# Moving ScalarE's preparation of heads and chunks to other places of an attention iteration

## The chip, the cores and the metric

The kernel runs on one core of one Trainium2 chip. A core has a matrix engine (TensorE, PE in the profile, with its weight loads as PEld), a vector engine (VectorE, DVE), an activation engine (ScalarE, ACT), a general engine (GpSimd, POOL), and a sync engine (SyncE, SP) that issues nearly all DMA transfers here. Each engine takes its own instructions strictly in the order of the program; they wait for one another through semaphores. The metric is the device time of one execution in microseconds. The median of several runs is compared.

## The reference

Three stages follow one another. The first is attention in which each query keeps only its 32 largest scores:

```python
scores = scale * np.matmul(q, k.transpose(0, 1, 3, 2))          # B, H, S, D = 4, 8, 576, 64
kth = np.partition(scores, -32, axis=-1)[..., -32:-31]
attn = softmax(np.where(scores >= kth, scores, -1e9))
x = np.matmul(attn, v)                                          # to (2304, 512)
h = x @ w_in                                                    # d_ff = 2048
x = (np.maximum(h, 0) + alpha * np.minimum(h, 0)) @ w_out
logits = x @ w_gate + modality_bias[modality_id]                # 8 experts, one for each token
out[mask] = gate_w * (np.maximum(x[mask] @ w1[e], 0) @ w2[e])   # F = 1024
```

## The kernel before, in words

Matrix products need more precision than one f16 holds, so an operand is scaled by a power of two and split into a high f16 part (ScalarE copies) and a low f16 part (GpSimd subtracts). Three products of parts then make one product.

**The iterations.** Attention is worked off in 72 iterations `s_` of two tiles of 128 queries each; an iteration is a pass of the loop in `phase1`. Tile `t` goes through it as a pipeline: its scores and its 32 largest values are found in iteration s (`topk`, VectorE, some 7 us), its mask in s+1 (`mask`: ScalarE writes `u`, line 526, from the thresholds `bc` that GpSimd has made, line 506; GpSimd subtracts, line 527), its exponentials in s+1 too (`expo`, line 530), its high part in s+1 (`high`, line 534), its low part in s+2 (`low`, lines 538 and 539, then a DMA transpose), and its product with V in s+3 (`av`).

**The order written out by hand.** The schedule is manual: the program order is the order on each engine. Within an iteration it is: hooks "early", `bc`, `low` of the tiles of s-2, `mask` of the tiles of s-1, squares and high parts of the FFN's weights (`wgroup.between`, in the first dozen iterations), hooks "next", the first five steps of `topk`, hooks "first", second products of the FFN (`mm2`), `pair` (ScalarE's high part of `g`, line 672, and GpSimd's low part, line 673), the scores of the next tiles, `mm1`, hooks "gap", the rest of `topk`, then on ScalarE `expo` of the first tile, `keep_scores` of the next tiles (line 457, which `topk` of the next iteration waits for), `expo` of the second tile, a copy of FFN values (line 651), `high`, then hooks "mid", `av`, hooks "late", and last the reading of weights (`wgroup`, VectorE, lines 259 to 261, and the weights' low parts, line 280 on GpSimd and 282 on VectorE).

**Preparation of heads.** A pair of heads (b, pr) is prepared once, by the list `c.steps` of `prep`: `load_qk` and `load_v` (SP), `norms_qk` and `norm_v` (ScalarE, line 392), `scales` (a small product on PE, then VectorE and GpSimd), `high_qk` (ScalarE, two instructions for q and two for k, lines 414 and 415), `low_qk` (GpSimd, line 419, two instructions), `high_v` (ScalarE, lines 431 and 432), `turn` (a DMA transpose from SP, line 423), `swap` (two DMAs from SP, line 427), `low_v`, `keep_`. The list `steps0` puts each step in a hook, so many iterations ahead of the pair's first tile: `("late", 4)` is the hook "late" four iterations ahead. Twelve pairs are prepared up to iteration 22, four more for iterations 54 to 63; all other pairs are loaded ready from memory. Before the main loop a short loop runs the hooks of iterations -6 to -2 alone.

**Preparation of chunks.** The output of attention is collected in chunks of 256 tokens for the FFN. A chunk's list `c.pre` puts `norm` (ScalarE, line 609), `scale` (VectorE, line 212, and GpSimd), `high` (ScalarE, lines 617 and 618, four instructions), `low` (GpSimd, line 622) and `turn` (DMA transpose) into hooks of the iterations after the chunk is complete. There are ten chunks; the first has a list of its own, `c.pre0`.

Of the kernel before, what the change touches and what calls it, by code (L numbers as in the profile page):

```python
# [10 lines left out]
F16 = mybir.dt.float16  # L11
# [3 lines left out]
AF = mybir.ActivationFunctionType  # L15
# [45 lines left out]
def tile_kernel(ctx, tc, q, k, v, w_in, w_out, alpha, mod_id, w_gate, mod_bias, w1, w2, out, dbg=None, force=False):  # L61
    nc = tc.nc
    V, A, G, T, SY = nc.vector, nc.scalar, nc.gpsimd, nc.tensor, nc.sync
# [95 lines left out]
    def run(exact):  # L159
        with ExitStack() as rs:  # L160
            rc = rs.enter_context(tc.tile_pool(name="rc", bufs=1))
            flags = None if exact else rc.tile([128, 2 * 144 + NFB], BF16, name="flags")
            ohs = rc.tile([128, E], F16, name="ohs")
            G.memset(ohs, 0.0)
            mp = Rec()
            with tc.manual_schedule():
                with ExitStack() as ph:
                    blk, over = phase1(exact, ph, rc, rs, flags, ohs, mp)
                mp.B = rs.enter_context(tc.tile_pool(name="moeB", bufs=1))
                if exact:  # L170
                    moe_phase(MAXBLK, blk, mp)
                else:
                    units_phase(blk, mp, lambda: doubts(rc, flags, blk, over))
            if not exact:
                return nc.values_load(blk[0:1, 32:33], min_val=0, max_val=(2 * 144 + NFB) * 128 + MAXBLK)


    def phase1(exact, ph, rc, rs, flags, ohs, mp):
        wts = ph.enter_context(tc.tile_pool(name="wts", bufs=1))
        atts = ExitStack()  # L180
        att = atts.enter_context(tc.tile_pool(name="att", bufs=2, side="right"))
# [15 lines left out]
        def hooked(slot, s_):  # L197
            while hooks[slot].get(s_):
                hooks[slot][s_].pop(0)()
# [25 lines left out]
        def flush():  # L225
            while fill:
                fill.pop(0)()
# [113 lines left out]
        def prep(m, b, pr, keep):  # L341

            c = Rec()
# [20 lines left out]
            raws = []  # L364
# [43 lines left out]
                fill.append(lambda: G.tensor_copy(c.sv[:, 0:1], c.s[:, 2:3]))  # L408
                fill.append(lambda: G.tensor_scalar(c.sv[:, 1:2], c.s[:, 2:3], 1e-9, None, op0=ALU.mult))

            def high_qk():
                c.qk = att.tile([128, 2, 9, 128], F16, name="qk", bufs=1)
                for i in range(2):
                    A.activation(raws[i], raws[i], AF.Copy, scale=c.s[:, i:i + 1])
                    A.activation(c.qk[:, i, :, 0:64], raws[i], AF.Copy)

            def low_qk():
                for i in range(2):
# [18 lines left out]
            def keep_():  # L437
                if keep:
                    SY.dma_start(qkD[b * 4 + pr].rearrange("p (s c) -> p s c", c=128), c.QK)
                    SY.dma_start(vvD[b * 4 + pr], c.VV.rearrange("p s c -> p (s c)"))  # L440

            c.steps = [load_qk, load_v, norms_qk, norm_v, scales, high_qk, low_qk, high_v, turn, swap, low_v, keep_]
            return c


# [150 lines left out]
        def chunk(ci, xn, rs):  # L596
            ffn = state.ffn
            c = Rec()
# [12 lines left out]
            def scale():  # L611
                c.s, c.iv = pow2(c.sq[:, :R], R, small, "xs", 5)
# [172 lines left out]
                        b0 = (2 * rs[0] + j) * S + 512  # L785
                        SY.dma_start(x2D[b0:b0 + 64, :], c.x2[64 * j:64 * j + 64, 0, :])

            c.pre = [("late", 0, norm), ("gap", 1, scale), ("late", 1, high), ("mid", 2, low), ("late", 2, turn)]
            c.pre0 = [("late", 0, norm), ("early", 1, lambda: (scale(), flush())), ("next", 1, high), ("gap", 1, low), ("mid", 1, turn)]
            c.mm1, c.relus, c.slope, c.pair, c.mm2 = mm1, relus, slope, pair, mm2  # L790
            c.fin, c.gate1, c.gate2, c.gate3, c.keep, c.place, c.logits, c.weight = fin, gate1, gate2, gate3, keep, place, logits, weight
# [68 lines left out]
        for n_, ts in enumerate(iters):  # L860
            for t in ts:
                first.setdefault(t.m, n_)
        pc = {}
        steps0 = [("next", 6), ("mid", 6), ("late", 6), ("next", 5), ("next", 4), ("late", 4), ("next", 3), ("late", 3),
                  ("late", 3), ("next", 2), ("mid", 2), ("late", 1)]
        seen = set()
        for m, (b, pr) in enumerate(seq):
            places = [("early", 3), ("late", 1)] if (b, pr) in seen else steps0
            seen.add((b, pr))
            for x, (slot, ahead) in enumerate(places):  # L870
                def step(m=m, x=x):
                    if m not in pc:
                        b_, pr_ = seq[m]
                        more = (b_, pr_) in seq[m + 1:]
                        pc[m] = prep(m, b_, pr_, more)
                    pc[m].steps[x]()
                at(slot, first[m] - ahead, step)
# [14 lines left out]
        def wstep(n):  # L892
            if state.out is not None or not n:
                return
            wgroup(n)
            if state.ffn is None and wgroup.cn["square"] == 32 and s_ > LCON[-1][1]:
                state.words.close()
                state.ffn = ph.enter_context(tc.tile_pool(name="ffn", bufs=2))
            if wgroup.cn["low"] == 32:
                state.stage.close()  # L900
                state.out = ph.enter_context(tc.tile_pool(name="ffnout", bufs=2))
# [14 lines left out]
        def start_chunk(ci, rs, s_):  # L916
            if state.ffn is None:
                return at("late", s_ + 1, lambda: start_chunk(ci, rs, s_ + 1))
            xn = xh.rearrange("p r h d -> p r (h d)") if ci == 8 else xns[ci // 2, ci % 2]
            if dbg is not None and exact == force:  # L920
                if ci < 8:
                    SY.dma_start(dbg[0][ci].rearrange("(p r) c -> p r c", r=2), xn)
                else:
                    SY.dma_start(dbg[0][ci].rearrange("(r p) c -> p r c", r=2)[:, rs[0]], xn[:, rs[0]])
            c = chunk(ci, xn, rs)
            c.k = state.started
            state.started += 1
            state.chunk = c
            for slot, x, f in (c.pre if c.k else c.pre0):
                at(slot, s_ + x, f)  # L930
            for fp in range(c.n):
                fpq.append((s_ + XLAT[c.k > 0], c, fp))
# [116 lines left out]
        for s_ in range(min(min(h_) for h_ in hooks.values() if h_), -LOOK):  # L1049
            hooked("early", s_)  # L1050
            wgroup.between(WSTEP)
            hooked("next", s_)
            hooked("mid", s_)
            flush()
            hooked("late", s_)
            wstep(WEARLY.get(s_, 0))
        s_ = -LOOK
        while True:
# [69 lines left out]
            while fpq and credit >= 1 and n_ < 2 and fpq[0][0] <= s_ and weights_for(fpq[0][2]):  # L1128
                credit -= 1
                _, c, fp = fpq.pop(0)  # L1130
# [446 lines left out]
```

## Time and profile before

| what | us |
|---|---|
| median of 3 runs (lowest, highest) | 1145.56 (1140.29, 1146.42) |
| the profiled execution: its time, and its span | 1142.26, 1140.5 |
| busy in the span: PE / DVE / ACT / POOL | 844.8 / 806.0 / 755.4 / 706.2 |
| first score tile on VectorE (iteration 0) | 39.74 |
| iterations 5 to 14 begin (first score instruction on VectorE) | 123.21, ..., 244.38 |
| iterations 23, 49 and 62 begin | 334.17, 553.83, 691.83 |
| last iteration (71) begins | 768.26 |

The span is from the first to the last instruction; the profiled execution's own time is 1.76 us longer. Busy time is an average over stages: after 768 us attention is nearly over and the FFN's end and the expert stage follow. A row of a timeline says when an instruction started, how long it ran, and in brackets how long its engine had stood idle before it and what released it.

### The profile page before, as it was taken

To read this page: it belongs to the slowest core of one execution; us is meant where nothing else is said; L and a number is where in the kernel's file an instruction comes from. 1 tells how busy PE (TensorE), PEld (TensorE's weight loads), DVE (VectorE), ACT (ScalarE), POOL (GpSimd) and SP (SyncE) were. 2 spreads that over 40 slices of the span, in tenths; PEclk is the share of its full clock that TensorE was granted. 3 is DMA by queue.
4 is the path that set the end of the run, shared out by engine and by line. 5 is a ranking of instruction groups with operands and counts; after the bars stand their busy time and mean duration, and the time that the engine had idled before them with its cause. 6 is when DMAs were issued, how large, how long until landed. Compare 5 with 4: busy or idle time off the path is not lost.

```text
span 1140.5 us, 21484 instructions
## 1 busy us (share of the span) xinstructions
PE 844.8 (74%) x7100; PEld 602.5 (53%) x7100; DVE 806.0 (71%) x2813; ACT 755.4 (66%) x1276; POOL 706.2 (62%) x1106
## 2 busy tenths in 40 slices
PE   0202133257779889778887878989999899999995
PEld 0001122135446566555555546657666778888884
DVE  5778778688799999999888879994225333443331
ACT  5466698998987887878888978895325233342441
POOL 3165397899988988988788999897333220230210
PEclk9999565678889999999899989999999999999998
DMA  8979967677795685686798678765104272543420
GB/s 248 257 181 230 269 141 157 160 164 165 169 214 126 133 180 108 132 175 122 138 161 167 154 155 178 161 130 74 19 20 167 93 258 84 176 147 112 130 93 21
DMA packets 297110, 170.21 MB, mean 149 GB/s; under 512 B 245458, under 2 KB 270034, under 8 KB 296988
## 3 DMA queue, kind: packets, MB, share of 16 engines
q1 hardware_dynamic: 293212, 158.24, 59.2%
q0 software_dynamic: 3776, 10.51, 2.5%
q8 instruction: 57, 0.93, 0.4%
q14 instruction: 65, 0.53, 0.2%
HBM read 81.42 MB, written 25.94 MB: 94 GB/s over the span
## 4 chain that ended last, share of the span: by engine, by line
PE 33%; POOL 17%; DVE 17%; ACT 16%; DMA 7%; issue 7%; SPq 2%; POOLq 0%; ACTq 0%
PE psS L1383 9%; PE psX L1366 8%; PE psX L686 6%; POOL HL L538 4%; POOL S L527 4%; PE psS L637 4%; DVE m L477 3%; DVE X L501 3%; ACT S L530 3%; DMA PT<-HL 3%; ACT HL L534 2%; ACT S L457 2%; DVE F L477 2%; DMA rawk<-in_k_dram 2%; ACT u L526 2%
## 5 line engine op out<-in xcount | busy, mean ns | idle before, releaser
L686 PE MATMUL psX<-Wo,g 128*128 128x512 f16 x864 | 218.2, 402 | 50.5 <-POOL g L673 36.0
L527 POOL TENSOR_TENSOR S<-u,S 128x576 f32<-128x576 bf16 x144 | 182.3, 1287 | 49.4 <-ACT u L526 49.2
L637 PEld LDWEIGHTS <-Wi 128*128 128x128 f16 x1920 | 170.9, 99 | 46.0 <-DVE gr L665 14.2
L538 POOL TENSOR_TENSOR HL<-S,HL 128x512 f16<-128x512 f32 x144 | 166.8, 1158 | 25.4 <-ACT HL L534 16.0
L637 PE MATMUL psH<-xT,Wi 128*128 128x256 f16 (+1 forms) x1488 | 158.4, 265 | 12.4 <-DVE gr L665 8.2
L453 PE MATMUL psS<-QK 128*128 128x512 f16 (+1 forms) x160 | 64.2, 439 | 137.4 <-DVE B L471 95.8
L686 PEld LDWEIGHTS <-g 128*128 128x128 f16 x864 | 82.4, 102 | 152.8 <-POOL g L673 46.1
L530 ACT ACTIVATE S<-S,bc,nb 128x576 f32<-128x576 f32 x144 | 124.1, 862 | 41.0 <-POOL S L527 41.0
L453 PEld LDWEIGHTS <-QK 128*128 128x128 f16 (+1 forms) x320 | 32.3, 110 | 196.5 <-issue 60.6
L1392 POOL DMA_INDIRECT out_dram<-o,ids x18 | 21.0, 1165 | 165.7 <-ACT o L1390 162.9
L673 POOL TENSOR_TENSOR g<-gr,g 128x512 f16<-128x512 f32 x72 | 84.0, 1167 | 53.4 <-ACT g L672 47.8
L477 DVE MAX8 m<-X 128x8 f32<-128x160 f32 x432 | 117.0, 312 | 0.0
L526 ACT ACTIVATE u<-S,bc 128x576 bf16<-128x576 f32 x144 | 103.1, 765 | 13.1 <-POOL bc L506 13.0
L1373 DVE SCALAR_TENSOR_TENSOR gl<-psX,gh 128x512 fp32r<-128x512 f32 (+1 forms) x40 | 25.4, 636 | 115.5 <-ACT gh L1372 115.5
L534 ACT ACTIVATE HL<-S 128x576 f16<-128x576 f32 x144 | 91.4, 681 | 15.6 <-DMA PT<-HL 15.6
L1372 ACT ACTIVATE gh<-psX 128x512 fp32r<-128x512 f32 (+1 forms) x40 | 22.3, 557 | 109.6 <-PE psX L1366 109.6
L457 ACT ACTIVATE S<-psS 128x576 f32<-128x576 f32 x144 | 84.2, 634 | 8.0 <-PE psS L454 8.0
L501 DVE MATCH_REPLACE8 X<-m,X 128x160 f32<-128x160 f32 x288 | 86.6, 307 | 0.0
L558 PE MATMUL bankO<-VV,PT 128*128 128x66 f16 (+1 forms) x2240 | 85.4, 199 | 0.0
L558 PEld LDWEIGHTS <-PT 128*128 128x128 f16 (+1 forms) x2240 | 81.8, 105 | 4.8 <-issue 3.5
L474 DVE SCALAR_TENSOR_TENSOR X<-psS,S 128x288 f32<-128x288 f32 (+1 forms) x144 | 80.7, 602 | 2.5
L672 ACT ACTIVATE g<-gr 128x512 f16<-128x512 f32 x72 | 44.9, 624 | 39.8 <-DVE gr L665 23.4
(286 smaller groups left out, 2069.6 us busy)
## 6 DMA issues: line engine op xcount, KB each, us to landing
raw<-in_moe_w_dram SPq DMA_DIRECT2D x40, 512.0 KB
qkD<-QK SPq DMA_DIRECT2D x16, 576.0 KB
QK<-qkD SPq DMA_DIRECT2D x16, 576.0 KB
wraw<-in_moe_w_in_dram SPq DMA_DIRECT2D x16, 512.0 KB
wraw<-in_moe_w_out_dram SPq DMA_DIRECT2D x16, 512.0 KB
vvD<-VV SPq DMA_DIRECT2D x16, 325.0 KB
VV<-vvD SPq DMA_DIRECT2D x16, 325.0 KB
K<-QK SPq DMA_DIRECT2D x32, 144.0 KB
```

What stands on the lines that cost most here:

```text
L457: A.activation(t.S, SC[:, t.z, :S], AF.Copy, scale=LOWER)
L477: ops.append(lambda: V.max(o, a_))
L501: ops.append(lambda i_=i_, r=r: V.match_replace(out=dst(i_), in_to_replace=m[:, i_, 8 * r:8 * r + 8], in_values=src(i_) if r == 0 else dst ...
L526: A.activation(u, t.S, AF.Relu, scale=-BIG, bias=t.cut)
L527: G.tensor_tensor(t.S, u, t.S, op=ALU.subtract)
L530: A.activation(t.S, t.S, AF.Exp, scale=t.c.negc, bias=t.b)
L534: A.activation(t.HL.rearrange("p a b -> p (a b)")[:, 0:S], t.S, AF.Copy)
L538: G.tensor_tensor(f[:, 640:1152], t.S[:, 0:512], f[:, 0:512], op=ALU.subtract)
L558: T.matmul(oo, l, r, start=(n_ == 0), stop=(n_ == len(ops) - 1), skip_group_check=True)
L637: T.matmul(h[:, fb, :], Wi[:, 4 * cc + f0 // 512, wh, f0 % 512:f0 % 512 + 128], c.xT[:, :R, xh_, cc, :], start=(n == 0), stop=(n == 11))
L686: T.matmul(c.X2[r], g[:, gh, fb, r * 128:r * 128 + 128], Wo[:, FB * fp + fb, wh, :], start=(fp == 0 and fb == 0 and n == 0), stop=(fp == c ...
L1383: T.matmul(self.Y[r], g_[:, r * 128:r * 128 + 128], w_[:, j % 2, :], start=(j == 0 and n == 0), stop=(j == 7 and n == 2))
```

## The change

It changes in which hook the steps of preparation stand, and cuts `high_qk` in two (`high_q`, `high_k`, the same four instructions). For a pair of heads the norms of q and k move from the end of iteration -6 to behind the masks of iteration -5, the norm of v from there to "mid" of -5, the high part of q from "late" to "mid" of -4, the high part of k from "late" of -4 to behind the masks of -3, the low parts on GpSimd from "next" to "mid" of -3, the high part of v from "late" of -3 to behind the masks of -2. For a chunk, `norm` and `high` move from "late" to "next" of the following iteration. The loop ahead of the main loop gets one more `flush()`. No instruction is added or removed.

```diff
-            def high_qk():
-                c.qk = att.tile([128, 2, 9, 128], F16, name="qk", bufs=1)
-                for i in range(2):
-                    A.activation(raws[i], raws[i], AF.Copy, scale=c.s[:, i:i + 1])
-                    A.activation(c.qk[:, i, :, 0:64], raws[i], AF.Copy)
+            def high_(i):
+                if i == 0:
+                    c.qk = att.tile([128, 2, 9, 128], F16, name="qk", bufs=1)
+                A.activation(raws[i], raws[i], AF.Copy, scale=c.s[:, i:i + 1])
+                A.activation(c.qk[:, i, :, 0:64], raws[i], AF.Copy)
...
-            c.steps = [load_qk, load_v, norms_qk, norm_v, scales, high_qk, low_qk, high_v, turn, swap, low_v, keep_]
+            c.steps = [load_qk, load_v, norms_qk, norm_v, scales, high_q, high_k, low_qk, turn, high_v, swap, low_v, keep_]
...
-            c.pre = [("late", 0, norm), ("gap", 1, scale), ("late", 1, high), ("mid", 2, low), ("late", 2, turn)]
+            c.pre = [("next", 1, norm), ("gap", 1, scale), ("next", 2, high), ("mid", 2, low), ("late", 2, turn)]
...
-        steps0 = [("next", 6), ("mid", 6), ("late", 6), ("next", 5), ("next", 4), ("late", 4), ("next", 3), ("late", 3),
-                  ("late", 3), ("next", 2), ("mid", 2), ("late", 1)]
+        steps0 = [("next", 6), ("mid", 6), ("next", 5), ("mid", 5), ("next", 4), ("mid", 4), ("next", 3), ("mid", 3),
+                  ("late", 3), ("next", 2), ("next", 2), ("mid", 2), ("late", 1)]
...
             hooked("next", s_)
+            flush()
             hooked("mid", s_)
```

## Rows read from the trace of the kernel before

**Rows 1.** Busy time by stretch: bounds, length, busy (instructions) by engine, PEclk, DMA, GB/s.
```profile
39.74:123.21 83.47, 15.20 (x102) 8.26 (x102) 69.06 (x202) 48.85 (x92) 39.15 (x75) 0.94 0.88 224
123.21:244.38 121.17, 38.29 (x360) 25.96 (x360) 94.47 (x315) 109.50 (x196) 97.73 (x141) 0.59 0.70 170
244.38:334.17 89.79, 66.93 (x600) 41.57 (x600) 75.30 (x298) 80.14 (x135) 82.36 (x121) 0.89 0.77 175
334.17:553.83 219.66, 190.54 (x2013) 128.79 (x2014) 216.57 (x888) 177.68 (x293) 190.91 (x293) 0.98 0.69 143
553.83:691.83 138.00, 111.95 (x1189) 73.82 (x1187) 113.61 (x467) 114.77 (x197) 120.89 (x196) 0.91 0.79 161
```

**Rows 2.** Waits over the span: total us, times, longest.
```profile
POOL S L527 <- ACT u L526: 49.2, 14, 10.7
...
ACT u L526 <- POOL bc L506: 13.0, 9, 2.9
```

**Rows 3.** Timeline of ScalarE from 78 to 95 us.
```profile
78.18 0.76 ACT L414 ACTIVATE rawq<-rawq,scs 128x576 f32<-128x576 f32 x1
...
79.56 0.76 ACT L414 ACTIVATE rawk<-rawk,scs 128x576 f32<-128x576 f32 x1
...
87.40 0.68 ACT L392 ACTIVATE junk<-rawq 128x576 f16<-128x576 f32 x1 [6.37 <-DMA rawq<-in_q_dram]
...
88.99 0.68 ACT L392 ACTIVATE junk<-rawk 128x576 f16<-128x576 f32 x1 [0.81 <-DMA rawk<-in_k_dram]
...
89.67 1.43 ACT L526 ACTIVATE u<-S,bc 128x576 bf16<-128x576 f32 x2
...
94.74 0.85 ACT L530 ACTIVATE S<-S,bc,nb 128x576 f32<-128x576 f32 x1
```

**Rows 4.** Timeline of GpSimd at three of its masks.
```profile
90.51 2.53 POOL L527 TENSOR_TENSOR S<-u,S 128x576 f32<-128x576 bf16 x2 [10.74 <-ACT u L526]
...
563.32 2.53 POOL L527 TENSOR_TENSOR S<-u,S 128x576 f32<-128x576 bf16 x2 [5.29 <-ACT u L526]
...
586.25 2.54 POOL L527 TENSOR_TENSOR S<-u,S 128x576 f32<-128x576 bf16 x2 [2.74 <-ACT u L526]
```

**Rows 5.** Timeline of ScalarE from 557 to 566 us.
```profile
557.15 0.68 ACT L392 ACTIVATE junk<-rawq 128x576 f16<-128x576 f32 x1 [1.02 <-DMA rawq<-in_q_dram]
...
559.93 0.71 ACT L617 ACTIVATE xn<-xn,xss 128x512 f32<-128x512 f32 x1
...
562.48 1.42 ACT L526 ACTIVATE u<-S,bc 128x576 bf16<-128x576 f32 x2
...
565.05 0.85 ACT L530 ACTIVATE S<-S,bc,nb 128x576 f32<-128x576 f32 x1
```

**Rows 6.** Timeline of SP's queue, ScalarE and VectorE in the start.
```profile
20.89 4.44 SPq L423 DMA_TRANSPOSE QK<-qk  x1
...
21.77 0.63 ACT L266 ACTIVATE junk<-Wi 128x512 f16<-128x512 f32 x1
...
39.74 0.47 DVE L474 SCALAR_TENSOR_TENSOR psS<-psS,S 128x288 f32<-128x288 f32 x1 [5.52 <-ACT S L457]
```

**Rows 7.** Timeline of ScalarE, GpSimd and VectorE from 652 to 657 us.
```profile
652.59 0.77 ACT L414 ACTIVATE rawq<-rawq,scs 128x576 f32<-128x576 f32 x1
...
654.97 0.20 POOL L506 TENSOR_TENSOR bc<-m,nb 128x4 f32<-128x4 f32 x1
...
655.37 0.61 ACT L609 ACTIVATE xjunk<-xn 128x512 f16<-128x512 f32 x1
...
656.11 0.15 DVE L212 TENSOR_SCALAR xsk<-xsq 128x1 int32<-128x1 int32 x1 [1.10 <-ACT xjunk L609]
...
656.74 1.43 ACT L526 ACTIVATE u<-S,bc 128x576 bf16<-128x576 f32 x2
```

**Rows 8.** Two lines' instructions: duration ns least/median/most, first and last start.
```profile
L419 POOL TENSOR_TENSOR qk<-rawq,qk x16: 1272/1280/1767, 18.2 to 660.5; 128x576 f16<-128x576 f32 x16
...
L282 DVE SCALAR_TENSOR_TENSOR Wi<-Wi,wp0s x6: 750/751/1778, 134.2 to 163.7; 128x512 f16<-128x512 f32 x6
```

More of the change, by code (lines that the diff above doesn't have):

```diff
@@ L409, in scales, with high_q, high_k @@
                 fill.append(lambda: G.tensor_scalar(c.sv[:, 1:2], c.s[:, 2:3], 1e-9, None, op0=ALU.mult))
-            def high_qk():
-                c.qk = att.tile([128, 2, 9, 128], F16, name="qk", bufs=1)
-                for i in range(2):
-                    A.activation(raws[i], raws[i], AF.Copy, scale=c.s[:, i:i + 1])
-                    A.activation(c.qk[:, i, :, 0:64], raws[i], AF.Copy)
+            def high_(i):
[3 more added lines that the diff above has]
+                A.activation(c.qk[:, i, :, 0:64], raws[i], AF.Copy)
+            def high_q():
+                high_(0)
+            def high_k():
+                high_(1)
             def low_qk():
```

## The prediction

> **What bounds the kernel now.** I read the busy time by stretch first, because the change touches only attention's first 62 iterations, and those have different limits. After iteration 23, from 334 to 554 us, VectorE is busy 216.57 of 219.66 us [rows 1]: nothing that ScalarE does earlier can shorten that stretch, and only something that makes VectorE wait can lengthen it. Preparation of heads runs in the other four rows. From 39.7 to 123 us VectorE has 69.06 of 83.47 us and the DMA engines a share of 0.88. From 123 to 244 us ScalarE is the fullest (109.50 of 121.17), as it also makes the high parts of the FFN's weights. From 244 to 334 and from 554 to 692 us GpSimd is the fullest (82.36 of 89.79, 120.89 of 138.00), with ScalarE and VectorE not far behind [rows 1]. The idle time of the fullest engine is the ceiling of what a new order can give in a stretch: 14.4, 11.7, 7.4 and 17.1 us.
>
> The waits come next. GpSimd stands 49.2 us for the masks that ScalarE makes, 14 times, up to 10.7 us; ScalarE stands 13.0 us for GpSimd's thresholds before a mask, 9 times [rows 2]. The first is what the change can take away, the second what it can make longer: today the work that stands ahead of a mask fills the time until its thresholds are there.
>
> The timelines then say where the 49.2 us lie. At 81 us ScalarE has made the high parts of q and k and comes to the next pair's norms, whose rows have not landed: 6.37 and 0.81 us idle. The masks stand behind and start at 89.67 [rows 3], and GpSimd has waited 10.74 us for them [rows 4]. The same pattern stands three times in all (near 57, 90 and 128 us). At 557 to 562 us norms and a chunk's high parts stand ahead of the masks, and GpSimd waits 5.29 us; at 586 us 2.74 [rows 4, 5].
>
> **The change part by part.** No instruction is added, so ScalarE's and GpSimd's totals stay. Prices are differences of starts on ScalarE: a high part of q or k 1.4 us (78.18 to 79.56), the two norms 1.5 without their waits [rows 3]; a chunk's high parts 2.55 [rows 5], its norms 1.4 [rows 7]. The low parts on GpSimd are two of 1.28 us [rows 8].
>
> *The start.* The high part of k now stands behind two squares of weights, of which the second runs at 21.77 to 22.40; today all high parts are done early enough that SP's transpose leaves at 20.89 [rows 6]. High k and its low part behind 22.40 end at 22.40 + 1.4 + 1.3 = 25.1: the transpose leaves up to 4.2 us later, and everything queued behind it on SP (the swap, the next pair's loads) with it. VectorE waits 5.52 us there for its first scores [rows 6], so a delay counts. Nothing if the squares come earlier once the second pair's norms are out of their way. I take +1.5, bounds 0 and +4.2.
>
> *Masks ahead of norms that wait for a load* (near 57, 90 and 128 us). ScalarE's idle time up to 87.40 can now take the masks and the squares, which today need 89.67 to about 94.0. The exponentials at 94.74 can start up to 4.3 us earlier [rows 3]. The squares need weights that VectorE is still reading, so I take 3.5 at 90 and 3.5 at 128, and nothing at 57, where VectorE does not wait for scores: -7 in all. Bounds: -13 (three times 4.3), under the ceiling of 14.4 [rows 1], and 0, if the DMA engines, not SP's order, set the landing.
>
> *Masks that now wait with work behind them.* At 652.59 ScalarE begins the high parts; the thresholds come at 654.97 + 0.20, so 2.6 us are filled today. After the change only the high part of q stays ahead of the mask: ScalarE idles 1.2 us, and the high part of k and the chunk's norms, 2.8 us together, stand between the mask and the exponentials, behind which the next scores are copied. The chunk's first square, for which VectorE already waits 1.10 us at 656.11, ends some 2.5 us later [rows 7]. Such late thresholds cost time where ScalarE sets the pace: I count four of them from 123 to 244 us, less what norm_v gives back by moving behind the copies, +3; one and a chunk's late norm from 244 to 334 us, +3, against -2 because GpSimd's low part of g no longer stands behind the two low parts of q and k, +1. From 554 to 692 us they are hidden behind GpSimd. Bounds 0 and +16 (13 iterations with preparation by 1.2 us).
>
> *The long stretch* from 334 to 554 us has only chunk steps. The norms end about where VectorE asks for them; 0, bounds 0 and +1.5 (three chunks by 0.5).
>
> *From 554 to 692 us.* At 557 the masks can start at 556.1 instead of 562.48; behind them come norms (the load of k still ends near 559.3) and the chunk's high parts, to about 562.5, then the high part of g: exponentials near 563.0 instead of 565.05, -2.0 [rows 5]. At 586.25 GpSimd's idle 2.74 us go, but the low part of g now waits for ScalarE's high part of g, which stands behind the moved pieces: -2. A smaller wait of this kind near 637 gives -1. Sum -5; bounds -9 (all three waits) and +2.
>
> **Sum**: 1.5 - 7 + 3 + 1 + 0 - 5 = -6.5 us. Against the profiled execution, 1142.26 us (span 1140.5 and 1.76 around it), that is 1135.8. This run lies 3.3 us under the median of 1145.56, so I put the forecast at 1145.56 - 6.5 = **1139 us**.
>
> One thing speaks against the move of GpSimd's low parts to mid-iteration. Six low parts of weights on VectorE take 750 ns at the median and 1778 at most, and the low part of q takes 1280 and once 1767 [rows 8]: the two stretch when they meet. The new place is just ahead of where VectorE's low parts run. [...]
>
> **The rivals.**
> *Larger gain.* The waits of [rows 4] vanish with nothing in their place: the bounds -13 and -9, with 0 elsewhere: about 1124 us. Against it: in the same iterations the moved pieces still stand ahead of the exponentials.
> *Only the order changes.* Two engines that are 83 to 92% full keep their sums, the exponentials come when the same pieces are done, and the early landing is set by the DMA engines. Then 1.5 + 0 + 3 + 1 - 5, about 1146.
> [...]
> *Slower.* The mask is a head of line: whenever its thresholds come later than ScalarE's previous piece ends, the pieces behind it wait. From the point at which those (up to 1.4 + 1.5 + 0.5) outlast GpSimd's own low parts and first subtraction, some 4 us, the exponentials move out. With the upper bound +16, the start at +4.2, the early gain 0 and the late one -5: about 1161, and about 1155 with two thirds of the bound. For it: 2.6 us filled in [rows 7]. Against it: the 13.0 us are few [rows 2], and GpSimd is not the limit everywhere.
>
> **The numbers.** Chances: forecast 0.48 (1132 to 1142), larger gain 0.10 (1120 to 1130), only the order 0.17 and the port 0.07 (both 1142 to 1149), slower 0.18 (1150 to 1162). A run of this kernel tells 0.5% (5.7 us) from no change; a fifth of the forecast's case lies inside that. Faster 0.10 + 0.38 = 0.48, same 0.10 + 0.24 = 0.34, slower 0.18. The likeliest case alone spans 1132 to 1142; for eight in ten I reach from 1123 to 1152, which leaves out the lowest of the larger gains and most of the slower case.
>
> **What would show it.** Right: GpSimd's wait for masks falls from 49.2 us to under 15, the two waits near 90 and 128 us are gone, iteration 5 begins some 5 us before 123.21 and iteration 12 gains little more; the two long iterations from 554 us shrink by 2 to 4 us together with GpSimd's waits there. ScalarE's wait for thresholds grows from 13.0 us to about 25. The stretch from 334 to 554 us keeps its length. Wrong: VectorE's first scores later than 43 us; the stretch from 244 to 334 us longer than 95; ScalarE's wait for thresholds over 35; or the loads at 80 to 130 us landing as much later as the masks come earlier.

## The result, and the profile of the changed kernel

The changed kernel took 1129.82 us (median of 4 runs, 1129.04 to 1134.75) against 1142.92 for the kernel before (4 runs): a ratio of 0.9895, interval 0.9846 to 0.9944. Seven more runs on another chip gave 0.9931 (0.9908 to 0.9955). The change is worth 0.7 to 1.1%, 6 to 13 us; forecast were 6.5. As a time, 1129.82 us lies below the 1132 to 1142 of the forecast's case, in the 1120 to 1130 of the larger gain.

The profiled execution is the slowest of its four: 1134.75 us, span 1133.0. Against the profiled execution of before (1142.26) that is 7.5 us less, but hardly a term of the sum sits where it was put. The windows of the changed kernel, cut where the same iterations begin (columns as in [rows 1]; the first two rows are iterations 0 to 5 and 5 to 14, the others 14 to 23, 23 to 49, 49 to 62 and the time behind iteration 71):

```profile
38.92:121.05 82.13, 15.77 (x104) 8.85 (x104) 69.10 (x201) 51.40 (x100) 43.20 (x79) 0.84 0.93 240
121.05:232.71 111.66, 39.25 (x358) 26.36 (x358) 91.88 (x316) 105.00 (x185) 93.25 (x136) 0.57 0.75 182
232.71:324.70 91.99, 69.30 (x602) 43.00 (x602) 74.62 (x296) 82.44 (x139) 82.41 (x121) 0.83 0.82 172
324.70:544.53 219.83, 189.30 (x2012) 128.09 (x2013) 216.65 (x889) 177.54 (x293) 191.30 (x294) 0.98 0.70 142
544.53:685.21 140.68, 113.17 (x1189) 74.91 (x1187) 113.70 (x466) 114.97 (x197) 121.43 (x196) 0.90 0.74 161
...
761.69:1133.00 371.31, 348.62 (x2065) 274.04 (x2064) 143.02 (x306) 135.49 (x207) 94.60 (x135) 0.98 0.35 107
```

Against [rows 1]: 83.47 became 82.13, 121.17 became 111.66, 89.79 became 91.99, the long stretch kept its length (219.66, 219.83), and 138.00 became 140.68. So most of the gain came between iterations 5 and 14; the stretch that was to give 5 us lost 2.7. How much of such differences is scatter is told at `x12_before`.

The waits over the span:

```profile
POOL g L679 <- ACT g L678: 57.0, 22, 5.6
...
ACT u L532 <- POOL bc L512: 11.0, 11, 2.8
...
POOL S L533 <- ACT u L532: 6.8, 4, 5.7
```

GpSimd's wait for masks fell from 49.2 us to 6.8, and ScalarE's wait for thresholds did not grow: 13.0 before [rows 2], 11.0 now. GpSimd's wait for the high part of `g` grew from 47.8 us (14 times) to 57.0 (22 times).

ScalarE in the changed kernel, where it stood 6.37 us for a load before [rows 3]:

```profile
77.90 1.42 ACT L532 ACTIVATE u<-S,bc 128x576 bf16<-128x576 f32 x2
...
82.33 0.63 ACT L266 ACTIVATE junk<-Wo 128x512 f16<-128x512 f32 x1 [1.33 <-DVE Wo L261]
...
84.38 0.63 ACT L266 ACTIVATE junk<-Wo 128x512 f16<-128x512 f32 x1 [1.34 <-DVE Wo L261]
...
85.01 0.76 ACT L414 ACTIVATE rawk<-rawk,scs 128x576 f32<-128x576 f32 x1
...
87.45 0.68 ACT L392 ACTIVATE junk<-rawk 128x576 f16<-128x576 f32 x1 [0.29 <-DMA rawk<-in_k_dram]
...
88.13 0.85 ACT L536 ACTIVATE S<-S,bc,nb 128x576 f32<-128x576 f32 x1
```

The masks start at 77.90 instead of 89.67, the squares, paced by VectorE's reading of the weights, fill the time until the load, the norms wait 0.29 us for it, and the exponentials start at 88.13 instead of 94.74: 6.6 us earlier. One iteration on they start at 128.48 instead of 136.58.

### The profile page after: what moved, and what is told of

It is laid out like the page before. It is cut to its first block, busy times and chain, and to the rows that moved or that the text cites. A ratio compares the mean times of both kernels' runs of the same rounds, so it can differ in the third digit from the quotient of the medians.

```text
span 1133.0 us, 21475 instructions
## 1 busy us (share of the span) xinstructions
PE 848.1 (75%) x7100; PEld 605.4 (53%) x7100; DVE 805.0 (71%) x2813; ACT 755.2 (67%) x1276; POOL 707.0 (62%) x1106
## 4 chain that ended last, share of the span: by engine, by line
PE 34%; DVE 24%; POOL 12%; ACT 12%; DMA 7%; issue 7%; SPq 3%; ACTq 0%; POOLq 0%
PE psS L1391 9%; PE psX L1374 8%; PE psX L692 6%; DVE X L507 5%; DVE m L483 5%; PE psS L643 4%; DVE F L483 3%; POOL HL L544 3%; POOL S L533 2%; DMA PT<-HL 2%; DVE gr L671 2%; PE psH L643 2%; ACT HL L540 2%; ACT S L536 1%; DVE X L480 1%
## 5 line engine op out<-in xcount | busy, mean ns | idle before, releaser
L692 PE MATMUL psX<-Wo,g 128*128 128x512 f16 x864 | 215.0, 399 | 15.3 <-POOL g L679 7.4
L643 PE MATMUL psH<-xT,Wi 128*128 128x256 f16 (+1 forms) x1488 | 160.2, 267 | 13.5 <-DVE gr L671 10.9
L679 POOL TENSOR_TENSOR g<-gr,g 128x512 f16<-128x512 f32 x72 | 83.5, 1160 | 62.5 <-ACT g L678 57.0
L532 ACT ACTIVATE u<-S,bc 128x576 bf16<-128x576 f32 x144 | 103.4, 768 | 11.7 <-POOL bc L512 11.0
L222 PE MATMUL bankO<-sq,ones 128*128 128x3 f32 x32 | 9.1, 355 | 104.1 <-ACT junk L392 92.8
```

The costliest lines, as they stand in the source:

```text
L532: A.activation(u, t.S, AF.Relu, scale=-BIG, bias=t.cut)
L643: T.matmul(h[:, fb, :], Wi[:, 4 * cc + f0 // 512, wh, f0 % 512:f0 % 512 + 128], c.xT[:, :R, xh_, cc, :], start=(n == 0), stop=(n == 11))
L692: T.matmul(c.X2[r], g[:, gh, fb, r * 128:r * 128 + 128], Wo[:, FB * fp + fb, wh, :], start=(fp == 0 and fb == 0 and n == 0), stop=(fp == c ...
```

## The experiments

**Which part of the change gains.** Three kernels do one part alone; all keep the one more `flush()` ahead of the main loop.

`x1_norms`: the list of before with only the norms moved.

```diff
-        steps0 = [("next", 6), ("mid", 6), ("late", 6), ("next", 5), ("next", 4), ...
+        steps0 = [("next", 6), ("mid", 6), ("next", 5), ("mid", 5), ("next", 4), ...
```

> The kernel before with one part of the change alone: the norms of a head pair (norms_qk to 'next' of -5, norm_v to 'mid' of -5); all else as before. Theory A (masks ahead of norms that wait for their load): this part alone carries most of the gain; iteration 14 begins 6 to 9 us before 244.4, GpSimd's wait for masks falls from 49.2 us to under 20, and the median is 5 to 9 us below the kernel before. Theory B (the gain comes from the high parts being spread over the iteration): iteration 14 begins at most 3 us earlier and the median is within 3 us of the kernel before.

Measured: 1136.32 us, ratio 0.9946 (0.9925 to 0.9966). Iteration 0 begins 2.6 us earlier than before, iteration 9 11.6, iteration 14 14.0; iterations 14 to 23 take 93.8 us (89.8 before), 49 to 62 140.9 (138.0). The early gain is the norms', all of it. GpSimd's wait for masks fell to 26.5 us, not under 20 as I had expected: the high parts still stand ahead of masks. What is given back later comes with the norms too, but not by one wait: in iterations 49 to 62 GpSimd stands 8.2 us for masks here and 1.5 for `g`.

`x2_highs`: only the high parts, `low_qk` and `high_v` at their new places.

```diff
-        steps0 = [..., ("next", 4), ("late", 4), ("next", 3), ("late", 3), ("late", 3), ("next", 2), ("mid", 2), ...
+        steps0 = [..., ("next", 4), ("mid", 4), ("next", 3), ("mid", 3), ("late", 3), ("next", 2), ("next", 2), ("mid", 2), ...
```

> The kernel before with the high parts, GpSimd's low parts and the high part of v moved as in the change, but the norms of heads and the chunks left where they were. Theory A: ScalarE's idle time ahead of the masks for a load remains, GpSimd still waits over 25 us for masks, iteration 14 begins at most 4 us before 244.4, the median is 0 to 4 us lower. Theory B: iteration 14 begins 6 to 10 us earlier and the median is 6 to 10 us lower.

Measured: 1143.51 us, ratio 1.0007 (0.9990 to 1.0023). The first scores come 3.65 us late, the delay that I had bounded at 4.2; iteration 9 is 0.3 late and iteration 14 on time. GpSimd still waits 40.8 us for masks. VectorE's first scores in this kernel, which waited 5.52 us before [rows 6]:

```profile
43.39 0.47 DVE L480 SCALAR_TENSOR_TENSOR psS<-psS,S 128x288 f32<-128x288 f32 x1 [6.80 <-ACT S L463]
```

`x3_chunks`: only the chunks' norms and high parts moved.

```diff
-            c.pre = [("late", 0, norm), ("gap", 1, scale), ("late", 1, high), ("mid", 2, low), ("late", 2, turn)]
+            c.pre = [("next", 1, norm), ("gap", 1, scale), ("next", 2, high), ("mid", 2, low), ("late", 2, turn)]
```

> The kernel before with the chunks' part of the change alone (norm and high of a chunk from 'late' to 'next'). Both theories: nothing before 215 us, the median within 3 us of the kernel before. If it is the chunks' part that lengthens the stretch of iterations 49 to 62 (138.0 us before, 140.7 after the whole change), the stretch is 139 to 142 us here; if it is the heads' part, it is 135 to 138 us, since a chunk's high parts leave the masks near 560.

Measured: 1137.43 us, ratio 0.9956 (0.9937 to 0.9976), 4.7 us less where I had expected under 3. Iterations 49 to 62 took 137.8 us, so it is not the chunks' part that lengthens them. In the trace attention is only 2.1 us earlier at iteration 71; the rest comes behind it, where I had expected nothing. The same drain instruction of ScalarE in the kernel before (iteration 71 begins at 768.26) and in this one (766.18):

```profile
793.80 0.69 ACT L693 ACTIVATE x<-psX,un 128x512 f32<-128x512 f32 x1 [2.86 <-PE psX L686]
```

```profile
790.75 0.69 ACT L699 ACTIVATE x<-psX,un 128x512 f32<-128x512 f32 x1 [2.86 <-PE psX L692]
```

25.54 us after the start of iteration 71 before, 24.57 here: 1.0 us less in the drain. It is 24.6 us in all ten profiles with the chunks moved; why is not shown. Another 1.7 us is TensorE's clock, 76 us behind iteration 71. First before, then here (columns as in [rows 1]):

```profile
844.00:847.50 3.50, 3.50 (x10) 1.25 (x9) 2.61 (x10) 0.63 (x1) 1.15 (x1) 0.53 0.02 5
```

```profile
842.00:845.50 3.50, 3.50 (x30) 2.75 (x29) 1.61 (x5) 0.35 (x1) 1.15 (x1) 1.00 0.02 5
```

TensorE is full in both, but does 10 matmuls in the one and 30 in the other. The granted clock is 0.50 of full speed in the half microseconds from 844.50 to 847.50. The group of 12 matmuls there:

```profile
843.33 4.44 PE L686 MATMUL psX<-Wo,g 128*128 128x512 f16 x12
```

```profile
840.28 2.75 PE L692 MATMUL psX<-Wo,g 128*128 128x512 f16 x12
```

This 1.7 us can't be put down to the chunks: `x2_highs`, with the chunks at their old places, has no such drop either, and an execution with the chunks moved can have one elsewhere (last section). So the profiles show 1.0 us behind attention and up to 2.1 in it; what else makes up the 4.7 us is open.

**Whether the parts add.** `x6_norms_chunks` has the norms and the chunks new, the high and low parts of heads old (`steps0` as in `x1_norms`, `c.pre` as in `x3_chunks`).

> The heads' norms and the chunks' pieces at their new places; the high parts of q, k and v and the low parts of q and k at their old ones. If the parts add, it takes -5.9 and -4.7 from the kernel before: a ratio near 0.991, some 1132 us, no worse than the whole change, and iteration 0 begins some 2.6 us earlier than before. If the parts need one another (the high parts have to move so that the norms' gain is kept), it stays at 1136 to 1137, the value of either part alone.

Measured: 1132.06 us, ratio 0.9926 (0.9901 to 0.9951), that of the whole change on the same chip. The high parts were not needed for the gain. Whether the two parts add fully (0.991) or not, the interval does not say.

**GpSimd's low parts.** `x4_low_back` is the changed kernel with `low_qk` back in "next".

```diff
-        steps0 = [..., ("mid", 4), ("next", 3), ("mid", 3), ...
+        steps0 = [..., ("mid", 4), ("next", 3), ("next", 3), ...
```

> The changed kernel with one thing undone: GpSimd's low parts of q and k back in 'next' of -3, behind the high part of k in the same hook. Theory P (GpSimd's subtraction of g no longer stands behind them, so the second products come earlier): PE's wait for GpSimd's g goes back from about 7 us to over 25, and the median is 2 to 5 us above the changed kernel. Theory Q (PE is not the bound there, and the low parts' new place beside VectorE's weight parts costs as much): the median is within 2 us of the changed kernel, on either side.

Measured: 1131.36 us, ratio 0.9896 (0.9872 to 0.9919): as fast as the change or somewhat faster. TensorE's wait for `g` was 12.9 us (36.0 before, 7.4 in the changed kernel), not over 25. Low parts longer than 1.4 us: 3 of 32 here, 3 of 32 in the changed kernel, 2 of 32 before. Where they stand made no difference to that. But iterations 49 to 62 took 136.5 us here.

**The stretch that grew.** `x5_again` is the changed kernel unaltered.

> The changed kernel once more, unaltered. It asks two things. The size: 1.1% below the kernel before (ratio 0.9895 in four runs, interval 0.9846 to 0.9944) should stand, with an interval of half the width: 0.988 to 0.992. And the stretch from iteration 49 to 62, which took 138.0 us before and 140.7 us in the profiled execution of the changed kernel. Theory one, the pieces that now stand ahead of ScalarE's high part of g lengthen it: 140 to 141 us again. Rival, that execution met something of its own, since the kernel with the low parts of q and k moved back took 136.5: 136 to 137.5 us here.

Measured: 1132.66 us, ratio 0.9931 (0.9908 to 0.9955), a smaller gain than the 0.988 to 0.992 that I expected; the same stretch took 142.5 us, and 139.4 in `x8_start`, whose order is the same there. So it is a property of the order, not of one execution. ScalarE and then GpSimd there, in the changed kernel:

```profile
547.49 1.43 ACT L532 ACTIVATE u<-S,bc 128x576 bf16<-128x576 f32 x2
...
550.51 0.68 ACT L392 ACTIVATE junk<-rawk 128x576 f16<-128x576 f32 x1 [0.93 <-DMA rawk<-in_k_dram]
...
551.19 0.71 ACT L623 ACTIVATE xn<-xn,xss 128x512 f32<-128x512 f32 x1
...
553.74 0.61 ACT L678 ACTIVATE g<-gr 128x512 f16<-128x512 f32 x1
...
554.26 0.85 ACT L536 ACTIVATE S<-S,bc,nb 128x576 f32<-128x576 f32 x1
```

```profile
554.43 1.15 POOL L679 TENSOR_TENSOR g<-gr,g 128x512 f16<-128x512 f32 x1 [2.29 <-ACT g L678]
...
566.39 1.17 POOL L679 TENSOR_TENSOR g<-gr,g 128x512 f16<-128x512 f32 x1 [1.66 <-ACT g L678]
...
578.11 1.17 POOL L679 TENSOR_TENSOR g<-gr,g 128x512 f16<-128x512 f32 x1 [1.33 <-ACT g L678]
579.23 0.19 POOL L687 TENSOR_TENSOR un<-xsi,cw 128x1 f32<-128x1 f32 x1
579.37 1.28 POOL L425 TENSOR_TENSOR qk<-rawq,qk 128x576 f16<-128x576 f32 x1
```

The masks are early, and between them and `g` stand norms with their wait and a chunk's high parts, 4.9 us; GpSimd, the fullest engine here, stands for `g`. At 578 it stands 1.33 us with two low parts of 1.28 us behind it that it could have done. In `x4_low_back` they come first, and `g` has no wait:

```profile
574.96 1.29 POOL L425 TENSOR_TENSOR qk<-rawq,qk 128x576 f16<-128x576 f32 x1
576.19 1.29 POOL L425 TENSOR_TENSOR qk<-rawk,qk 128x576 f16<-128x576 f32 x1
577.43 1.17 POOL L679 TENSOR_TENSOR g<-gr,g 128x512 f16<-128x512 f32 x1
```

GpSimd's waits within iterations 49 to 62 (total, times, longest), before and then in the changed kernel:

```profile
POOL S L527 <- ACT u L526: 9.3, 3, 5.3
POOL HL L538 <- ACT HL L534: 4.0, 2, 2.9
```

```profile
POOL g L679 <- ACT g L678: 7.5, 7, 2.3
POOL HL L544 <- ACT HL L540: 7.2, 4, 2.0
```

The wait for masks fell to 0.4 us and that for `g`, which there was none of before, came in its place. The wait for ScalarE's high part of the exponentials (`HL`) grew besides. In `x7_gap` below they are 2.1 us for `g` and 4.4 for `HL`.

`x7_gap` moves three pieces behind ScalarE's part of `g`.

```diff
-        steps0 = [..., ("next", 5), ("mid", 5), ("next", 4), ("mid", 4), ("next", 3), ("mid", 3),
-                  ("late", 3), ("next", 2), ("next", 2), ("mid", 2), ("late", 1)]
+        steps0 = [..., ("gap", 5), ("mid", 5), ("next", 4), ("mid", 4), ("gap", 3), ("mid", 3),
+                  ("late", 3), ("gap", 2), ("next", 2), ("mid", 2), ("late", 1)]
...
             hooked("next", s_)
+            hooked("gap", s_)
             flush()
```

> The changed kernel with three pieces of a pair (norms of q and k, high part of k, high part of v) one hook later, behind ScalarE's high part of g instead of ahead of it. If the pieces ahead of g are what GpSimd and TensorE wait for, the wait of GpSimd's low part of g for ScalarE's falls from 57.0 us to near the 47.8 of before, iterations 14 to 23 shrink from 92.0 to about 90 us and 49 to 62 from 140.7 to 137 or 138, and the time is 2 to 5 us under the changed kernel's: 1125 to 1128. Rival: ScalarE stands idle for VectorE's slope ahead of g, which the pieces filled, and they now lie ahead of the exponentials alone: no change or 1 to 4 us slower.

Measured: 1127.78 us, ratio 0.9892 (0.9868 to 0.9917), 4.9 us under the changed kernel on the same chip. The wait fell to 49.1 us (15 times). Iterations 14 to 23 took 90.3 us, but 90.9 in `x5_again` too, so nothing is shown there. The stretch from iteration 49 fell to this:

```profile
541.51:677.11 135.60, 107.89 (x1189) 73.50 (x1187) 113.40 (x467) 114.61 (x197) 121.18 (x196) 0.94 0.78 164
```

`x11_norms_gap` moves only the norms behind `g`.

```diff
-        steps0 = [..., ("next", 5), ("mid", 5), ("next", 4), ...
+        steps0 = [..., ("gap", 5), ("mid", 5), ("next", 4), ...
```

> The changed kernel with only the norms of q and k behind ScalarE's high part of g; the high parts of k and of v stay ahead of it. If the norms are what delays g after iteration 49 (with the norms alone at their new place that stretch took 140.9 us, with the high parts alone 136.8), it takes 136 to 137.5 us here, as with all three pieces moved (135.6), and the time is 3 to 5 us under the changed kernel, a ratio to before near 0.990. If the high parts do it, it stays at 140 to 142 us and the ratio at 0.993.

Measured: 1129.25 us, ratio 0.9888 (0.9866 to 0.9909); the stretch 137.2 us. The norms make most of the difference there. Iterations 14 to 23 took 92.3 us; the two profiles of the changed kernel have 92.0 and 90.9, so the high parts' share there is not shown.

**The start.** `x8_start` puts the first pair's high and low parts back.

```diff
+            if m == 0:
+                places = steps0[:5] + [("late", 4), ("late", 4), ("next", 3)] + steps0[8:]
```

> The changed kernel with the first pair's high parts and low parts at their old places. Iteration 0 should begin 1.7 us earlier (37.2 instead of 38.9), as with the norms alone, because the high part of k no longer stands behind two squares of weights there. If the start counts, the time is 1 to 2 us below the changed kernel's; if, as with the high parts alone (3.65 us late at iteration 0, 0.3 at iteration 9), a delay of the start is taken up by the iterations that wait for loads, the time is that of the changed kernel within 1 us, and iteration 14 begins at the same time.

Measured: 1127.85 us, ratio 0.9892 (0.9867 to 0.9917). Iteration 0 begins at 37.07, 2.5 us before that of `x5_again`, and iteration 14 still 3.0 us before, so my second expectation failed here. In `x2_highs` the waits for loads took up a late start; that the change has removed those waits may be why, but `x9_gap_start` below lost the same lead. Another 3.1 us between the profiles of `x8_start` and `x5_again` lie in iterations 49 to 62, whose order is the same in both: not all of the 4.8 us between their medians is shown to be the start's.

**Both corrections.** `x9_gap_start` joins the last two edits; `x10_gap_low` has `high_k` and `low_qk` in "next" besides.

```diff
-        steps0 = [..., ("mid", 4), ("gap", 3), ("mid", 3), ...
+        steps0 = [..., ("mid", 4), ("next", 3), ("next", 3), ...
```

> Both edits on top of the changed kernel: the three pieces behind ScalarE's high part of g, and the first pair's high and low parts at their old places. Each alone came out some 4.9 us under the changed kernel on the same chip (1127.78 and 1127.85 against 1132.66). If they act in different stretches they add: in the trace iteration 9 begins 13 us earlier than in the kernel before and iteration 62 some 17 us earlier, and the time is 14 to 16 us under before, a ratio near 0.987. Rival: what each gained is partly the scatter between executions, and together they stay at 11 to 12 us, a ratio near 0.9895.

Measured: 1125.30 us, ratio 0.9851 (0.9827 to 0.9875), 16.3 us under before: the lowest time of all, though its interval meets those of `x7_gap`, `x8_start` and `x10_gap_low`. Its profile does not show the two gains adding, though: iteration 62 is 14.0 us earlier, where `x7_gap` alone has 14.7, because iterations 0 to 5 took 82.9 us and not 80.5. Whether the start adds is open.

> As the one above, but the high part of k and the low parts of q and k stand in the hook next, three iterations ahead. With the low parts back there alone, iterations 49 to 62 took 136.5 us, where three executions with them in mid-iteration took 139.4 to 142.5: GpSimd works them off while it would stand idle for ScalarE's high part of g. If that gain comes on top, iterations 49 to 62 fall to 133 to 134 us and the time to a ratio near 0.985. Rival: the pieces of norms and of the high part of v behind g have removed that idle time already, and the low parts now only delay GpSimd's low part of g: 135 to 137 us and no difference to the kernel above.

Measured: 1127.03 us, ratio 0.9874 (0.9851 to 0.9897); the stretch 135.5 us, as in `x9_gap_start` (135.4). The rival holds: with `g` in time there is no gap for the low parts to fill.

**How steady the stretches are.** `x12_before` is the kernel before once more.

> The kernel before once more, for a second profile. If the stretches are properties of the program order, its iterations 49 to 62 take 138.0 us again and 0 to 5 83.5, each within 1 us; what scatters should lie behind the last iteration, where executions of one kernel so far took 369.4 to 371.3 us.

Measured: 1142.54 us. Iterations 0 to 5 took 83.5, 23 to 49 221.0, 49 to 62 137.1, and 373.9 us lay behind the start of iteration 71 (372.3 in the other profile). Iterations 5 to 14 took 118.9 us, not 121.2; `x2_highs` and `x3_chunks` have 118.9 and 119.2 there. In the first profile one of VectorE's low parts of weights ran 4.31 us, while GpSimd went through four instructions without a gap; the same one ran 0.76 us in the second:

```profile
240.15 4.31 DVE L282 SCALAR_TENSOR_TENSOR Wo<-Wo,wp1s 128x512 f16<-128x512 f32 x1 [0.99 <-ACT Wo L274]
```

```profile
239.97 0.76 DVE L282 SCALAR_TENSOR_TENSOR Wo<-Wo,wp1s 128x512 f16<-128x512 f32 x1 [1.07 <-ACT Wo L274]
```

So differences of up to 2.2 us in a stretch are scatter here, and 3.1 us in iterations 49 to 62 of the changed kernel's order (139.4 to 142.5). What I rest on stands in several kernels. Iterations 5 to 14 took 111.6 to 112.5 us in the ten profiles with the norms moved and 118.9 to 121.2 in the four without. Iterations 49 to 62 took 139.4 to 142.5 us in the five profiles that have the norms ahead of `g` (`x4_low_back` aside), and 135.4 to 138.0 in the nine others.

## Why the prediction came out as it did

The forecast of 6.5 us lies at the lower end of what was measured (6.4 and 13.1), and the direction and the main mechanism were right: masks ahead of norms that wait for loads. But the terms were off by more than the sum, in both directions; that their sum came near is luck. The time of 1139 us was too high by the base as well: with a fourth run the median before is 1142.92, not 1145.56.

*The start*, +1.5: measured -0.8 (`x5_again` -0.2). The two parts are visible alone, -2.6 from the norms and +3.65 from the high parts, and do not simply add. The transpose leaves at 23.97 instead of 20.89 [rows 6], 3.1 of the 4.2 us that I had bounded, and earlier norms of the second pair make up for it.

*Masks ahead of norms*, -7: right in kind, too small. I let the exponentials follow at most 4.3 us earlier and took 3.5; they came 6.6 and 8.1 earlier. Near 90 us the norm of v, 0.74 us, has left the place ahead of them too, and the wait for the load ended 1.5 us earlier (87.45, not 88.99). Near 128 us the high parts of weights, which rows of 90 us could not show, fill the time as well: of the two waits for the load there, 6.52 and 0.89 us, nothing is left. From iteration 0 to 14 the profile gains 10.9 us, `x1_norms` 11.4, under the ceiling of 14.4 + 11.7; against `x12_before` it is 8.7 and 9.2.

*Masks that now wait*, +3: this step failed. I took out of ScalarE's queue what leaves the place ahead of a mask (the high part of k, the norms), but did not put in what comes: the high part of v, which stood ahead of the masks of the iteration before, now stands behind them. Iterations 6 and 7 show it, before and then in the changed kernel, with the two engines in order of time:

```profile
144.78 1.44 ACT L526 ACTIVATE u<-S,bc 128x576 bf16<-128x576 f32 x2 [2.79 <-POOL bc L506]
...
154.24 0.77 ACT L414 ACTIVATE rawq<-rawq,scs 128x576 f32<-128x576 f32 x1
...
156.42 0.20 POOL L506 TENSOR_TENSOR bc<-m,nb 128x4 f32<-128x4 f32 x1
```

```profile
135.91 1.44 ACT L532 ACTIVATE u<-S,bc 128x576 bf16<-128x576 f32 x2 [2.78 <-POOL bc L512]
...
141.65 0.81 ACT L437 ACTIVATE rawv<-rawv,scs 128x640 f32<-128x640 f32 x1
...
146.86 0.76 ACT L414 ACTIVATE rawq<-rawq,scs 128x576 f32<-128x576 f32 x1
...
147.56 0.20 POOL L512 TENSOR_TENSOR bc<-m,nb 128x4 f32<-128x4 f32 x1
```

From the masks to the next thresholds it is 11.6 us in both. But ScalarE comes to the high part of q 1.5 us later, by the length of the high part of v, and that fills the time that I had put down as idle. At the place of [rows 7], in the changed kernel, ScalarE, then GpSimd:

```profile
647.93 0.68 ACT L415 ACTIVATE qk<-rawq 128x576 f16<-128x576 f32 x1
648.52 1.43 ACT L532 ACTIVATE u<-S,bc 128x576 bf16<-128x576 f32 x2
649.86 0.76 ACT L414 ACTIVATE rawk<-rawk,scs 128x576 f32<-128x576 f32 x1
```

```profile
647.49 0.21 POOL L512 TENSOR_TENSOR bc<-m,nb 128x4 f32<-128x4 f32 x1
```

The thresholds start 0.35 us after the high part of q begins (647.14), not 2.4 us after it as before, and the mask follows without idle time. Here too they come no earlier after the masks before (10.3 and 10.2 us); ScalarE is 2.1 us later, with waits of 1.12 and 0.68 us for TensorE on its way. The wait stayed at 11.0 us where I had forecast about 25. The slower rival rested on the same step.

*From 244 to 334 us*, +1: +2.2 in the profile, +1.0 in `x5_again`. *The long stretch*, 0: 0.2.

*From 554 to 692 us*, -5: the second step that failed; +2.7 and +4.5. I had seen that `g` would stand behind the moved pieces, and charged it to one iteration only. GpSimd's idle time moved from the masks (9.3 to 0.4 us) to `g` (none to 7.5) and to the high part of the exponentials (4.0 to 7.2), and `x7_gap` gets it back by moving the pieces once more (135.6).

*Behind attention*: no term at all. The chunks' part gains 1.0 us in the drain, in each of the ten profiles with it. The drops of the clock are another matter. Over the first 90 us after the start of iteration 71 the ten profiles with the chunks moved have none, and the four without have two, two, one and none; but seven of the ten have one in iterations 62 to 71, which then take 78.1 us instead of 76.5. That the change prevents drops is not shown.

*The rivals.* The larger gain came nearest in the early part (8.7 to 10.9 us of its 13); in the late part its 9 us became a loss. *Only the order changes* is refuted by `x1_norms`, and the loads that were to hold the gain back came earlier: the second norm's wait ended at 87.45, not 88.99 [rows 3]. *The low parts side by side*, the 0.07 among the chances: in the first profile of the kernel before one of the two does stretch in each of the five places where they meet. At 163.71 and 210.97 us VectorE's low part of weights ran 1.78 us while GpSimd made a low part of k (1.27 us from 163.67 and from 210.93), and the two low parts of q that began while VectorE's ran took 1.74 and 1.77 us (161.96 and 209.20). The fifth is the 4.31 us at 240.15, with low parts of q and k at 239.17 and 240.41, a longer stretch than the 1778 ns of [rows 8], which holds six of the sixteen. But a loss by the move, for which that chance stood (eight instructions, each of which stretches another by 1.0 us), no run shows: 3 of 32 low parts of q and k are stretched at either place, and of VectorE's 16 low parts of weights 4 ran over 1.4 us in the changed kernel, 5 and 3 in the two profiles of before, so the move cost nothing there. What the move to mid-iteration did cost was GpSimd's order ahead of `g`.

Of the signs that I named, the masks' wait, the length of the long stretch and the first scores ahead of 43 us came true; iteration 5 gained 2.2 us and not 5, and iteration 12 10.8, because the second of the two waits falls behind the start of iteration 5. The two long iterations from 554 us (49 and 51) shrank by 1.5 and 1.3 us, but the iteration behind each grew by 2.0 and 2.4.

## What to carry to other kernels

When pieces move around a wait, write out the whole queue between the wait before and this one, what comes in as well as what goes out, before you price idle time: here a piece that came in filled it. Then follow the in-order queue to the next handover behind the moved pieces (here `g`) and ask who stands for that; a piece belongs ahead of a wait only if no partner waits for what it now delays. And compare the whole span, in more than one profile: a part priced at nothing gave 1.0 us behind the stages that it touches, and a drop of the clock that another execution of the same order does not have looked like 1.7 more.

## What was not expected of the hardware

TensorE's clock fell to 0.50 while TensorE was busy without a gap (844.50 to 847.50 us), with 0.30 us of idle time in the seven microseconds ahead, just before the fp32 matmuls of the gate. The kernel with the chunks moved has the same work and the same 0.30 us, and keeps 1.00. These two stretches don't tell what decided. Two executions of the changed kernel itself part in the same way in iteration 63, the first profile and then `x5_again`:

```profile
696.08 2.75 PE L692 MATMUL psX<-Wo,g 128*128 128x512 f16 x12 [2.28 <-ACT gr L706]
```

```profile
696.28 4.43 PE L692 MATMUL psX<-Wo,g 128*128 128x512 f16 x12 [2.27 <-ACT gr L706]
```

The matmuls and the idle time just ahead are the same; the granted clock is 1.00 in the first and 0.50 in the second. Such drops, 1.7 us each where TensorE is the bound, are a part of the scatter between executions of one kernel.

In the slow iterations from 49 to 62 the clock is lower as well (0.90 in the mean, 0.94 in `x7_gap`), but it was 0.91 and 0.90 in the two profiles of the kernel before. It isn't the whole cause: iteration 52 takes 11.5 us at 0.70, 10.2 at 1.00 in `x7_gap` and 10.2 at 0.83 in `x8_start`. How much of the late `g` acts through the clock stays open.
